# Attention and max-out MoE on one core: W2 ahead of batch 0 in the load queue, x^T of batch 1 on TensorE, and fixed PSUM pools

## The chip, the cores and the metric

The kernel runs on one core of one Trainium2 chip. The metric is the device time of one execution in microseconds. The profile is one execution taken by the hardware profiler; its times count from the start of its span.

## What is computed

Inputs are x (8 batches, 8 heads, 512 rows, 64 wide), state (8, 8, 32, 64) and the weights w1, w2 (512 x 1024) and w_out (1024 x 512), all fp32. The reference, cut to what matters:

```
scores = scale * x @ state^T;    a  = softmax(scores);   xread = a @ state
scores2 = scale * state @ x^T;   a2 = softmax(scores2);  sread = a2 @ x
X = concat(xread, sread over the rows), heads side by side    # 4352 x 512
out = maximum(X @ w1, X @ w2) @ w_out
```

The kernel uses max(h1, h2) = h2 + relu(h1 - h2), so out = X (W2 Wo) + relu(X (W1 - W2)) Wo. For the rows of xread it folds the state S into the weights: X W = a (S W), so that the 512-deep product becomes one of depth 256 (8 heads by 32 states).

## The kernel before, in words

The order of the work on each engine is written out by hand (`manual_schedule`): every engine takes its instructions in the order of the program, and waits where data or a buffer is missing. All loads stand in SP's queue: states of batches 0 to 2, batch 0, then half 0 of W2, two quarters of Wo, half 1 of W2, the other two quarters, both halves of W1, batch 1, the other states, batch 2.

Per batch there are these steps (names of the functions):
- `cast_x` (L180) makes a bf16 copy xp of x, which `u_sr` needs; `u_xt` (L197) transposes xp on TensorE and copies x^T out of PSUM. For later batches `compact_x` (L187) casts into a packed tile xc, and `d_xt` (L194) transposes that by DMA from SP's queue.
- `u_exp` (L210) and `u_norm` (L226): scores, exp on ACT, then reduce, reciprocal and multiply, which give a. `u_at` (L256, TensorE) or `d_at` (L251, DMA) make a^T, the tile aT.
- `u_sr` (L235), `u_srt` (L266): the rows of sread and their transpose into sread_t.
- `sw_mm`/`u_sw` (L275, L289): S W in three chunks of 512 columns. Chunks 0 and 1 are S (W1 - W2). For the first batches they are S W1 plus (-S) W2 from the cast weights (`two`), for the others they come from wcat, which `w_sub` (L387) fills on POOL. Chunk 2 is S (W2 Wo). ACT and VectorE copy the results to swt.
- `l1` (L305): 8 blocks of two matmuls each, a relu after each, by turns on ACT and VectorE. `l2_open`, `l2_add`, `l2_close` (L317 to L333): four output blocks, with 2 + 8 matmuls each.

The weights: `w_cast`, `wo_cast` cast them, `w_t` (L399) transposes W2 on TensorE into w2t, and `w_wo` (L411) builds W2 Wo in four quarters as the quarters of Wo come. L442 to L519 interleave this with batch 0 and with the start of batch 1. From L521 on each batch runs l1 and l2 with the next batch's steps put between the blocks (`fillers`, L420): exps and casts after l1, `u_sr` after l2's first block, S W and the DMA transposes after the third.

[...] Up to L520 there are two pools of four, `ps` for all and `acc` for W2 Wo and l2. Then `one_ring` (L62) closes both and opens one pool of eight. `warm_up` (L133) issues matmuls on zeros.

Of the kernel before, what the change touches and what calls it, by code (L numbers as in the profile page):

```python
# [15 lines left out]
def kernel(  # L16
# [14 lines left out]
    nc = tc.nc  # L31
# [5 lines left out]
    NC = S // 128  # L37
# [10 lines left out]
    keep = ctx.enter_context(tc.tile_pool(name="keep", bufs=2))  # L48
    big = ctx.enter_context(tc.tile_pool(name="big", bufs=2))

    early = ctx.enter_context(ExitStack())
    pools = dict(ps=early.enter_context(tc.tile_pool(name="ps", bufs=4, space=bass.MemoryType.PSUM)),
                 acc=early.enter_context(tc.tile_pool(name="acc", bufs=4, space=bass.MemoryType.PSUM)))
    ctx.enter_context(tc.manual_schedule())

    def bank(dtype=F32, kind="ps"):
        return pools[kind].tile([128, 512 if dtype == F32 else 1024], dtype, tag="b", name=kind)

    def acc():
        return bank(kind="acc")  # L60

    def one_ring():  # L62
        early.close()
        pools["ps"] = pools["acc"] = ctx.enter_context(tc.tile_pool(name="ring", bufs=8, space=bass.MemoryType.PSUM))

    def copy(eng, o, i):
        if eng == "A":
# [23 lines left out]
    def load_states(bs):  # L91
        nc.sync.dma_start(out=s_f[:, 2 * bs.start:2 * bs.stop],
                          in_=state[bs].rearrange("b (q h) n d -> (h n) (b q) d", q=2))
# [6 lines left out]
    def load_w(t, w, ch):  # L100
        cs = slice(ch * 512, (ch + 1) * 512)
        nc.sync.dma_start(out=t[:, :, cs], in_=w.rearrange("(i p) f -> p i f", p=128)[:, :, cs])

    def load_wo(q):
        nc.sync.dma_start(out=wof[:, 2 * q:2 * q + 2],
                          in_=moe_w_out.rearrange("(k p) n -> p k n", p=128)[:, 2 * q:2 * q + 2])

    load_states(first)
    load_x(0)
    for ch in range(2):  # L110
        load_w(w2f, moe_w2, ch)
        load_wo(2 * ch)
        load_wo(2 * ch + 1)
    load_w(w1f, moe_w1, 0)
    load_w(w1f, moe_w1, 1)
    load_x(1)
    load_states(slice(3, 8))
    load_x(2)

    ident = consts.tile([128, 128], BF16)  # L120
# [12 lines left out]
    def warm_up(n):  # L133
        p = bank()
        for k in range(n):
            nc.tensor.matmul(p, warm[:, 0:128], warm, start=(k == 0), stop=(k == n - 1))  # L136
# [28 lines left out]
    def negate_states():  # L165
        for g in range(2):
            gs = slice(64 * g, 64 * g + 64)
            negate("V", sneg[gs], sbd[gs, 0:TWO, g::2, g, :])
# [25 lines left out]
    def d_xt(b):  # L194
        nc.sync.dma_start_transpose(out=st[b]["xt"], in_=st[b]["xc"].rearrange("p h w -> p (h w)"))

    def u_xt(b, g, eng):  # L197
        d = st[b]
        p = bank(BF16)
        for i in range(4):  # L200
            for c in range(NC):
                k = 2 * i + c // 2
                nc.tensor.transpose(p[64 * (c % 2):64 * (c % 2) + 64, k * 128:(k + 1) * 128], d["xp"][:, 2 * i + g, c, 0:64], ident)
        copy(eng, d["xt"].rearrange("p (i g u) t -> p g i (u t)", g=2, u=2)[:, g], p.rearrange("p (i w) -> p i w", i=4))
# [5 lines left out]
    def u_exp(b, g):  # L210
        d = st[b]
        if g == 0:
            d["e"] = at.tile([128, 2, 4, NC, Ns], BF16, tag="e", name="e")
            d["es"] = at.tile([128, 2, 4 * NC], F32, tag="es", name="es")
            d["er"] = at.tile([128, 2, 4 * NC], F32, tag="er", name="er")
            d["a"] = at.tile([128, 2, NC, 4, Ns], BF16, tag="a", name="a")
        p = bank()
        for i in range(4):
            for cp in range(2):
                k = 2 * i + cp  # L220
                nc.tensor.matmul(p[:, k * 64:k * 64 + 64],  # L221
                                 d["xt"][:, 4 * i + 2 * g + cp, :], sbd[:, b, 2 * i + g].rearrange("p u n -> p (u n)"),
                                 start=(k == 0), stop=(k == 7))
        nc.scalar.activation(out=d["e"][:, g].rearrange("p i c n -> p (i c n)"), in_=p, func=ACTF.Exp, scale=scale)  # L224

    def u_norm(b, g, mul):  # L226
        d = st[b]
        nc.vector.tensor_reduce(d["es"][:, g], d["e"][:, g].rearrange("p i c n -> p (i c) n"),  # L228
                                axis=mybir.AxisListType.X, op=ALU.add)
        nc.vector.reciprocal(d["er"][:, g], d["es"][:, g])  # L230
        mul.tensor_mul(  # L231
            d["a"][:, g].rearrange("p c i n -> p i c n"), d["e"][:, g],
            d["er"][:, g].rearrange("p (i c) -> p i c", i=4).unsqueeze(3).to_broadcast([128, 4, NC, Ns]))
# [39 lines left out]
    swt = consts.tile([128, 2, 2, WC], BF16)  # L273

    def sw_mm(b, ch, engs="VA"):  # L275
        pg = [bank(), bank()]
        two = b < TWO and ch < 2 and (b, ch) != (1, 0)
        terms = ((sbd, w1b), (sneg, w2b)) if two else ((sbd, wcat),)
        for k, (sv, w) in enumerate(terms):
            for i in range(4):  # L280
                for g in range(2):
                    gs = slice(64 * g, 64 * g + 64)
                    nc.tensor.matmul(pg[g][32 * i:32 * i + 32, :],  # L283
                                     sneg[gs, b, i, :] if k else sbd[gs, b, 2 * i + g, g, :],
                                     w[gs, i, ch * 512:(ch + 1) * 512],
                                     start=(k == 0), stop=(k == len(terms) - 1))
        return lambda: [copy(engs[g], SW[b][:, g, ch * 512:(ch + 1) * 512], pg[g]) for g in range(2)]
# [99 lines left out]
    def w_sub(q):  # L387
        cs = slice(q * 256, (q + 1) * 256)
        nc.gpsimd.tensor_sub(wcat[:, :, cs], w1f[:, :, cs], w2f[:, :, cs])  # L389

    def w_cast(o, w, ch, engs="VA"):
        cs = slice(ch * 512, (ch + 1) * 512)
        for k in range(2):
            copy(engs[k], o[:, 2 * k:2 * k + 2, cs], w[:, 2 * k:2 * k + 2, cs])

    def wo_cast(q, eng):
        copy(eng, wo[:, 2 * q:2 * q + 2], wof[:, 2 * q:2 * q + 2])

    def w_t(ch, half, eng):  # L399
        p = bank(BF16)  # L400
        for j in range(2):
            for k in range(4):
                f = 4 * ch + k
                nc.tensor.transpose(p[:, (4 * j + k) * 128:(4 * j + k + 1) * 128],
                                    w2b[:, 2 * half + j, f * 128:(f + 1) * 128], ident)
        copy(eng, w2t[:, 2 * half:2 * half + 2, 4 * ch:4 * ch + 4, :].rearrange("p j f t -> p j (f t)"),
             p.rearrange("p (j t) -> p j t", j=2))
# [3 lines left out]
    def w_wo(q, i):  # L411
        if q == 0:
            WO[i] = acc()
        for f in range(2 * q, 2 * q + 2):
            nc.tensor.matmul(WO[i], w2t[:, i, f, :], wo[:, f, :], start=(f == 0), stop=(f == NF - 1))  # L415
        if q == 3:
            copy("V" if i % 2 else "A", wcat[:, i, FF:WC], WO[i])
# [21 lines left out]

    for b in range(B):  # L440
        SW[b] = swt[:, b % 2]
    warm_up(6)  # L442
    cast_states("V", first)
    states(first)
    warm_up(5)
    cast_x(0, (("V", slice(0, 4, 2)), ("A", slice(4, 8, 2)), ("V", slice(1, 4, 2)), ("P", slice(5, 8, 2))))
    u_xt(0, 0, "V")
    u_xt(0, 1, "A")
    u_exp(0, 0)
    u_exp(0, 1)  # L450
    w_cast(w2b, w2f, 0, "VV")
    wo_cast(0, "P")
    wo_cast(1, "P")
    warm_up(1)
    w_t(0, 0, "A")
    w_t(0, 1, "A")
    u_norm(0, 0, nc.vector)
    u_sr(0)
    u_norm(0, 1, nc.vector)
    negate_states()  # L460
    warm_up(3)
    for q in range(2):
        for i in range(4):
            w_wo(q, i)
    w_cast(w2b, w2f, 1)
    wo_cast(2, "P")
    w_t(1, 0, "V")
    w_t(1, 1, "A")
    u_at(0, "V")
    u_srt(0)  # L470
    wo_cast(3, "V")
    for i in range(4):
        w_wo(2, i)
    w_cast(w1b, w1f, 0)
    w_sub(0)
    w_sub(1)
    for i in range(4):
        w_wo(3, i)
    u_sw(0, 0)
    u_sw(0, 2)  # L480
    l1(0, {}, range(0, 4))
    for c in range(NC):
        l2_open(0, c)
    w_cast(w1b, w1f, 1)
    compact_x(1, 0)
    compact_x(1, 1)
    d_xt(1)
    cast_x(1)
    w_sub(2)
    w_sub(3)  # L490
    cast_states("P", rest)
    load_x(3)
    sT = d_states(rest)
    l2_add(0, 0, range(0, 4))
    u_sw(0, 1)
    for c in range(1, NC):
        l2_add(0, c, range(0, 4))
    l1(0, {}, range(4, 8))
    u_sc(1, 0, nc.vector)
    u_sc(1, 1, nc.gpsimd)  # L500
    cast_x(2)
    l2_add(0, 0, range(4, 8))
    l2_close(0, 0)
    u_sw(1, 0)
# [6 lines left out]
    l2_add(0, 2, range(4, 8))  # L511
    l2_close(0, 2)
    u_at(1, "V")
    l2_add(0, 3, range(4, 8))
    l2_close(0, 3)
    d_xt(2)
    u_sw(1, 2)
    u_srt(1)
    l2_out(0)  # L519
    one_ring()  # L520
    for b in range(1, B):  # L521
        fill = fillers(b)
        if b + 2 < B:
# [39 lines left out]
```

The softmax here doesn't subtract the row's maximum and nothing guards it: scores larger than these inputs give would overflow.

## Time and profile before

| | |
|---|---|
| time, median of 4 runs | 155.28 us (154.96 to 156.66) |
| the profiled execution | 155.36 us |
| its span | 153.5 us |
| TensorE busy | 141.2 us, 92% |
| VectorE, ACT, POOL busy | 83.7, 75.5, 43.6 us |
| DMA | 29.89 MB, mean 195 GB/s; 385 GB/s and over from 8 to 22 us |
| l1 of batch 0 starts | 25.17 us |
| l1 of batches 1, 2, ..., 7 starts | 42.39, 56.35, 70.31, 85.43, 100.65, 115.09, 129.05 us |

In lines of the timeline the first two numbers are start and length in us, then come engine, source line, operation, out<-in, shape and count; in brackets stands the idle time just before and what ended it. PE is TensorE's matmul, PEld its weight load, DVE VectorE, SPq the issue of a DMA from SP's queue. "ps" and "acc" are PSUM tiles. In the DMA view q1 is the queue of the kernel's own transfers and q8 one of two that carry instructions.

### The profile page before, as it was taken

The numbers are of one execution on the slowest core, as the hardware profiler recorded it, in microseconds if no ns is written. First come the engines' busy times: TensorE is split into PE (matmuls) and PEld (weight loads), VectorE is DVE, ScalarE is ACT, GpSimd is POOL, SyncE is SP. The second block draws the span as 40 slices with busy tenths as digits, with TensorE's granted clock in tenths as the row PEclk, the third lists the DMA queues.
The fourth block names the chain that finished last, engine by engine and source line by source line (L and its number), as shares of the span: only waits on it lengthen the run. The fifth ranks groups of instructions, "written<-read, shape, count | busy, mean of one in ns | idle before, by whom it ended". The sixth has DMA issues, their size and how long they took to land. (4 is left out here: it accounts for less than half of the span.)

```text
span 153.5 us, 3031 instructions
## 1 busy us (share of the span) xinstructions
PE 141.2 (92%) x1255; PEld 67.0 (44%) x1255; DVE 83.7 (55%) x151; ACT 75.5 (49%) x126; POOL 43.6 (28%) x44
## 2 busy tenths in 40 slices
PE   6769789999799999999999799979999999999990
PEld 1355533344345444534543354335434544664460
DVE  5379628528955486655556355635565546731120
ACT  3065519927864565756384637463747217621010
POOL 3025129994930910270064006300500050000000
PEclk9999999999999999999999999999999999999999
DMA  4999999999399298749849990990099015602423
GB/s 113 349 398 391 383 381 296 286 162 288 72 301 293 89 193 301 249 77 247 282 153 106 319 299 32 107 341 34 2 124 358 0 22 51 273 0 63 138 99 116
DMA packets 37934, 29.89 MB, mean 195 GB/s; under 512 B 24864, under 2 KB 33312, under 8 KB 37024
## 3 DMA queue, kind: packets, MB, share of 16 engines
q1 hardware_dynamic: 37776, 29.56, 69.3%
q8 instruction: 10, 0.16, 0.5%
q10 hardware_dynamic: 144, 0.13, 0.3%
q14 instruction: 4, 0.03, 0.1%
HBM read 15.20 MB, written 8.91 MB: 157 GB/s over the span
## 5 line engine op out<-in xcount | busy, mean ns | idle before, releaser
L326 PE MATMUL acc<-wo,r 128*128 128x512 bf16 x248 | 58.9, 379 | 0.0
L326 PEld LDWEIGHTS <-r 128*128 128x128 bf16 x248 | 23.9, 98 | 28.8 <-issue 0.6
L301 DVE TENSOR_SCALAR r<-ps 128x512 bf16<-128x512 f32 x32 | 22.1, 692 | 19.1 <-PE ps L311 19.0
L311 PE MATMUL ps<-aT,swt 128*128 128x512 bf16 x128 | 29.1, 379 | 3.3 <-DMA aT<-a 2.4
L231 POOL TENSOR_TENSOR a<-e,er 128x512 bf16<-128x512 bf16 x13 | 13.4, 1050 | 64.0 <-ACT e L224 32.2
L70 DVE COPY ob<-acc 128x512 f32<-128x512 f32 (+1 forms) x17 | 11.4, 671 | 27.4 <-PE acc L326 27.0
L299 ACT ACTIVATE r<-ps 128x512 bf16<-128x512 f32 x32 | 19.2, 599 | 10.9 <-PE ps L311 10.6
L311 PEld LDWEIGHTS <-swt 128*128 128x128 bf16 x128 | 12.0, 98 | 18.2 <-issue 3.3
L68 ACT CAST swt<-ps 128x512 bf16<-128x512 f32 x24 | 12.9, 592 | 12.6 <-PE ps L283 12.4
L322 PE MATMUL acc<-swt,aT 128*128 128x512 bf16 x62 | 18.1, 381 | 0.0
L68 ACT COPY ob<-acc 128x512 f32<-128x512 f32 (+1 forms) x16 | 9.2, 576 | 15.9 <-PE acc L326 10.9
L70 DVE CAST swt<-ps 128x512 bf16<-128x512 f32 x24 | 15.3, 681 | 1.8 <-PE ps L283 1.7
L72 POOL CAST xp<-xf 128x2048 bf16<-128x2048 f32 (+1 forms) x8 | 14.3, 1783 | 5.9 <-DMA xf<-in_x_dram 5.9
L224 ACT ACTIVATE e<-ps 128x512 bf16<-128x512 f32 x16 | 8.8, 595 | 14.0 <-PE ps L221 14.0
L68 ACT CAST xc<-xf 128x1024 bf16<-128x1024 f32 x14 | 13.9, 1050 | 0.0
L228 DVE TENSOR_REDUCE es<-e 128x16 f32<-128x512 bf16 x16 | 10.6, 662 | 1.8 <-ACT e L224 1.8
L389 POOL TENSOR_TENSOR wcat<-w1f,w2f 128x1024 bf16<-128x1024 f32 x4 | 9.8, 2477 | 3.0 <-DMA w1f<-in_moe_w_dram 3.0
L415 PE MATMUL acc<-wo,w2t 128*128 128x512 bf16 x32 | 7.2, 379 | 1.5 <-POOL wo L72 1.5
L322 PEld LDWEIGHTS <-aT 128*128 128x128 bf16 x62 | 4.7, 98 | 6.0 <-issue 2.6
L136 PE MATMUL ps<-warm 128*128 128x512 bf16 x15 | 5.9, 536 | 1.3 <-POOL warm L122 1.3
L283 PE MATMUL ps<-wcat,sbd 64*32 64x512 bf16 x168 | 6.7, 380 | 0.1
L221 PEld LDWEIGHTS <-xt 128*128 128x128 bf16 x128 | 4.7, 98 | 3.0 <-ACT xt L68 0.7
(68 smaller groups left out, 102.7 us busy)
## 6 DMA issues: line engine op xcount, KB each, us to landing
xf<-in_x_dram SPq DMA_DIRECT2D x8, 1024.0 KB, 8.5
out_dram<-ob SPq DMA_DIRECT2D x7, 1024.0 KB, 5.2
w2f<-in_moe_w_dram SPq DMA_DIRECT2D x2, 1024.0 KB, 10.2
wof<-in_moe_w_out_dram SPq DMA_DIRECT2D x4, 512.0 KB, 11.5
w1f<-in_moe_w_dram SPq DMA_DIRECT2D x2, 1024.0 KB, 15.7
out_dram<-ob SPq DMA_DIRECT2D x3, 256.0 KB, 2.8
out_dram<-obs SPq DMA_DIRECT2D x8, 64.0 KB, 1.7
s_f<-in_state_dram SPq DMA_DIRECT2D x1, 320.0 KB, 13.6
```

What stands on the lines that cost most here:

```text
L68: nc.scalar.copy(o, i)
L70: nc.vector.tensor_copy(o, i)
L72: nc.gpsimd.tensor_copy(o, i)
L224: nc.scalar.activation(out=d["e"][:, g].rearrange("p i c n -> p (i c n)"), in_=p, func=ACTF.Exp, scale=scale)
L228: nc.vector.tensor_reduce(d["es"][:, g], d["e"][:, g].rearrange("p i c n -> p (i c) n"), axis=mybir.AxisListType.X, op=ALU.add)
L231: mul.tensor_mul(d["a"][:, g].rearrange("p c i n -> p i c n"), d["e"][:, g], d["er"][:, g].rearrange("p (i c) -> p i c", i=4).unsqueeze(3) ...
L299: nc.scalar.activation(out=o, in_=p, func=ACTF.Relu)
L301: nc.vector.tensor_scalar(o, p, scalar1=0.0, scalar2=None, op0=ALU.max)
L311: nc.tensor.matmul(p, SW[b][:, g, f * 128:(f + 1) * 128], AT[b][:, g, :], start=(g == 0), stop=(g == 1))
L322: nc.tensor.matmul(OB[b][1 + c], AT[b][:, g, c * 128:(c + 1) * 128], SW[b][:, g, FF:WC], start=(g == 0), stop=False)
L326: nc.tensor.matmul(OB[b][1 + c], R[b][:, f, c * 128:(c + 1) * 128], wo[:, f, :], start=False, stop=(f == NF - 1))
L389: nc.gpsimd.tensor_sub(wcat[:, :, cs], w1f[:, :, cs], w2f[:, :, cs])
```

## The change

The load queue is led by half 0 of W2 and two quarters of Wo; the states and batch 0 come next, and the rest as before. The hand-written order follows: W2's transposes and the first two quarters of W2 Wo stand before batch 0's work on TensorE, more warm-up matmuls are put in (20 in place of 15), several casts change engine. Batch 1 has its x^T from TensorE (`u_xt`) with the casts split over VectorE and ACT, in place of `compact_x`, `d_xt` and a cast on POOL. Its exps stand inside l1 of batch 0, and chunk 0 of its S W comes from the cast weights. All four `w_sub` stand together, later. The two pools of four banks stay to the end; from batch 2 on the third chunk of S W takes its two banks from `acc`. In the order of instructions on TensorE the changed kernel has 2,600 weight loads and matmuls in place of 2,510, all 90 of them before l1 of batch 1.

```
-    early = ctx.enter_context(ExitStack())
-    pools = dict(ps=early.enter_context(tc.tile_pool(name="ps", bufs=4, space=bass.MemoryType.PSUM)),
-                 acc=early.enter_context(tc.tile_pool(name="acc", bufs=4, space=bass.MemoryType.PSUM)))
+    pools = {k: ctx.enter_context(tc.tile_pool(name=k, bufs=4, space=bass.MemoryType.PSUM)) for k in ("ps", "acc")}
...
-    def one_ring():
-        early.close()
-        pools["ps"] = pools["acc"] = ctx.enter_context(tc.tile_pool(name="ring", bufs=8, space=bass.MemoryType.PSUM))
...
+    load_w(w2f, moe_w2, 0)
+    load_wo(0)
+    load_wo(1)
     load_states(first)
     load_x(0)
-    for ch in range(2):
-        load_w(w2f, moe_w2, ch)
-        load_wo(2 * ch)
-        load_wo(2 * ch + 1)
+    load_w(w2f, moe_w2, 1)
+    load_wo(2)
+    load_wo(3)
     load_w(w1f, moe_w1, 0)
...
     def sw_mm(b, ch, engs="VA"):
-        pg = [bank(), bank()]
-        two = b < TWO and ch < 2 and (b, ch) != (1, 0)
+        pg = [bank(kind="acc" if ch == 2 and b > 1 else "ps") for g in range(2)]
+        two = b < TWO and ch < 2
...
-    warm_up(6)
+    warm_up(11)
+    w_cast(w2b, w2f, 0)
+    w_t(0, 0, "V")
+    w_t(0, 1, "A")
+    wo_cast(0, "P")
+    wo_cast(1, "P")
+    warm_up(3)
+    for i in range(4):
+        w_wo(0, i)
     cast_states("V", first)
     states(first)
-    warm_up(5)
+    negate_states()
+    for i in range(4):
+        w_wo(1, i)
     cast_x(0, (("V", slice(0, 4, 2)), ("A", slice(4, 8, 2)), ("V", slice(1, 4, 2)), ("P", slice(5, 8, 2))))
     u_xt(0, 0, "V")
     u_xt(0, 1, "A")
+    warm_up(2)
     u_exp(0, 0)
     u_exp(0, 1)
-    w_cast(w2b, w2f, 0, "VV")
-    wo_cast(0, "P")
-    wo_cast(1, "P")
-    warm_up(1)
-    w_t(0, 0, "A")
-    w_t(0, 1, "A")
     u_norm(0, 0, nc.vector)
+    w_cast(w2b, w2f, 1, "PA")
+    wo_cast(2, "P")
+    wo_cast(3, "P")
+    warm_up(4)
     u_sr(0)
     u_norm(0, 1, nc.vector)
-    negate_states()
-    warm_up(3)
-    for q in range(2):
-        for i in range(4):
-            w_wo(q, i)
-    w_cast(w2b, w2f, 1)
-    wo_cast(2, "P")
-    w_t(1, 0, "V")
-    w_t(1, 1, "A")
+    w_t(1, 0, "A")
+    w_t(1, 1, "V")
     u_at(0, "V")
     u_srt(0)
-    wo_cast(3, "V")
     for i in range(4):
         w_wo(2, i)
     w_cast(w1b, w1f, 0)
-    w_sub(0)
-    w_sub(1)
...
     l1(0, {}, range(0, 4))
+    w_cast(w1b, w1f, 1, "PA")
+    cast_x(1, (("V", slice(0, 4, 2)), ("V", slice(4, 8, 2)), ("A", slice(1, 4, 2)), ("A", slice(5, 8, 2))))
     for c in range(NC):
         l2_open(0, c)
-    w_cast(w1b, w1f, 1)
-    compact_x(1, 0)
-    compact_x(1, 1)
-    d_xt(1)
-    cast_x(1)
-    w_sub(2)
-    w_sub(3)
+    for q in range(4):
+        w_sub(q)
     cast_states("P", rest)
-    load_x(3)
-    sT = d_states(rest)
     l2_add(0, 0, range(0, 4))
     u_sw(0, 1)
-    for c in range(1, NC):
-        l2_add(0, c, range(0, 4))
-    l1(0, {}, range(4, 8))
-    u_sc(1, 0, nc.vector)
-    u_sc(1, 1, nc.gpsimd)
+    l2_add(0, 1, range(0, 4))
+    l2_add(0, 2, range(0, 4))
+    u_xt(1, 0, "V")
+    u_xt(1, 1, "A")
+    l2_add(0, 3, range(0, 4))
+    l1(0, {4: [lambda: u_exp(1, 0)], 5: [lambda: u_exp(1, 1)]}, range(4, 8))
+    u_norm(1, 0, nc.vector)
+    u_norm(1, 1, nc.gpsimd)
+    load_x(3)
     cast_x(2)
+    sT = d_states(rest)
...
     u_at(1, "V")
+    u_sw(1, 2)
     l2_add(0, 3, range(4, 8))
     l2_close(0, 3)
     d_xt(2)
-    u_sw(1, 2)
     u_srt(1)
     l2_out(0)
-    one_ring()
```

More of the change, by code (lines that the diff above doesn't have):

```diff
@@ L116 @@
     load_x(1)
-    load_states(slice(3, 8))
+    load_states(rest)
     load_x(2)
```

## Prediction

> **What bounds the kernel now.** I read the page first, then TensorE's waits, the windows by batch, the early timeline, and last the DMA view of two narrow windows. The page:
>
> ```profile
> span 153.5 us, 3031 instructions
> ...
> PE 141.2 (92%) x1255; PEld 67.0 (44%) x1255; DVE 83.7 (55%) x151; ACT 75.5 (49%) x126; POOL 43.6 (28%) x44
> ...
> q8 instruction: 10, 0.16, 0.5%
> ```
>
> TensorE is busy for 92% of the span, no other engine for more than 55%. So the question is where TensorE waits. Its waits (us in total, times, longest):
>
> ```profile
> PE ps L311 <- DMA aT<-a: 2.4, 3, 1.1
> PE acc L415 <- POOL wo L72: 1.5, 1, 1.5
> PE ps L203 <- DVE xp L70: 1.4, 1, 1.4
> ...
> PE ps L311 <- ACT sread_t L68: 0.8, 1, 0.8
> ```
>
> The largest lies in the late batches: l1 waits three times for the DMA transpose of a. The windows from one l1 to the next (length, then PE) price it:
>
> ```profile
> 42.39:56.35 13.96, 13.96 (x129) 6.41 (x130) 8.54 (x16) 7.40 (x12) 4.94 (x5) 1.00 0.85 223
> ...
> 70.31:85.43 15.12, 14.13 (x132) 6.40 (x131) 8.14 (x15) 8.81 (x16) 4.13 (x4) 1.00 0.81 191
> 85.43:100.65 15.22, 14.12 (x129) 6.37 (x130) 8.14 (x15) 8.16 (x14) 3.95 (x4) 1.00 0.82 191
> 100.65:115.09 14.44, 14.12 (x129) 6.38 (x130) 8.14 (x15) 7.74 (x13) 2.06 (x2) 1.00 0.53 124
> ```
>
> A clean batch takes 13.96 us with TensorE full; batches 3, 4 and 5 lose 1.16 + 1.26 + 0.48 = 2.9 us. The rest of the room is before 42.4 us. The timeline (start, length) has the points that my steps use:
>
> ```profile
> 7.56 0.62 ACT L68 CAST xp<-xf 128x512 bf16<-128x512 f32 x1 [5.54 <-DMA xf<-in_x_dram]
> ...
> 10.38 1.20 ACT L224 ACTIVATE e<-ps 128x512 bf16<-128x512 f32 x2
> ...
> 19.68 3.61 PE L415 MATMUL acc<-wo,w2t 128*128 128x512 bf16 x16 [1.47 <-POOL wo L72]
> ...
> 22.61 0.69 DVE L70 CAST w1b<-w1f 128x1024 bf16<-128x1024 f32 x1 [2.02 <-DMA w1f<-in_moe_w_dram]
> ...
> 32.74 1.89 PE L311 MATMUL ps<-aT,swt 128*128 128x512 bf16 x8
> ...
> 35.82 0.69 DVE L228 TENSOR_REDUCE es<-e 128x16 f32<-128x512 bf16 x1 [0.46 <-ACT e L224]
> ```
>
> **What the Trainium skill says.** "Runtime: NRT & Kernel Launch", Instruction fetch mechanics: an engine's instructions are fetched by a DMA queue of its own in 16 KiB blocks of 256. The trace agrees: 2 x 1255 TensorE instructions are 9.8 blocks, and q8 moved 10. The page calls the cost mostly hidden; here I doubt it. "DMA: Bandwidth & Descriptors", Queues, rings and completion order: each DMA engine consumes a ring in order and takes turns between rings packet by packet. The first half I use for the loads; the second the trace does not bear out cleanly, since some q8 packets started only when earlier transposes were through. Its section Latency and other measured facts gives DMA transposes 261 GB/s; aT's 256 KB would be 1.0 us as an estimate, but the trace has 3.2 from issue to landing, and that is used.
>
> **The q8 packets.** Narrow DMA windows find them at 83.3, 98.5, 111.6 and 125.5 us, the first three in just the three slow batches. In 80 to 86 us the transpose lands 5.0 us after issue, and in a window of a fast batch without q8, 66 to 70.5 us, 3.2:
>
> ```profile
> q8 instruction: 1, 0.02, 1.0%
> ...
> aT<-a SPq DMA_TRANSPOSE x1, 5.0
> ```
>
> ```profile
> aT<-a SPq DMA_TRANSPOSE x1, 3.2
> ```
>
> A clean batch issues aT 10.0 us after its l1 began (66.36 against 56.35), so 3.2 us leaves 0.7 to spare and 5.0 overruns by 1.1. That fits the 1.0 and 1.1 waited. Where DMA was idle, the packets started after 1938, 2195 and 2449 TensorE instructions, that is 256k less 110. A batch has 258 instructions, so a packet keeps its place in the batch: 10.4 to 10.9 us after l1 there, on top of aT. This is inferred from coincidence, not shown.
>
> **The change, part by part.**
> 1. Loads. The first five (192 + 1024 + 1024 + 512 + 512 KB) keep their sum and change their order, so batch 0 lands last of them, when the second Wo quarter landed before: at 13.0 instead of 7.5 us. Later loads keep their places; half 0 of W1 stays at 22.6. If lines of 2 KB start faster than batch 0's of 1 KB, it could be 12.1; I take 12.9.
> 2. Batch 0's chain. From batch 0's landing (7.54) to the end of the first exp (10.97) were 3.4 us; the norm block on VectorE, first reduce to last multiply, ran 11.48 to 15.23, 3.75 us. So a is whole at 12.9 + 3.4 + 3.75 + 0.1 = 20.15, and after transposes (0.4) the third quarter of W2 Wo starts at 20.6 instead of 19.68. Sixteen matmuls by 216 ns are 3.46: S W1 starts at 24.06. Before it waited for W1's cast until 22.61 + 0.69 + 0.06 = 23.36. Cost 0.7; the load's 5.4 us are otherwise hidden, because that time was spent waiting for Wo and W1. Half 0 of W2's cast, its transposes and the first two quarters of W2 Wo now run before 13 us under the same loads: nothing. Casts moved to POOL (1.04 each) end by 20.95, before the matmul wants them at 22.3: nothing.
> 3. Batch 1's x^T. Removed: two ACT casts (1.05 each), POOL's cast (2.06), SP's DMA transpose (its issue 2.10, ahead of load 3) and the wait for it, 0.6. Added: four casts of about 0.6 on VectorE and ACT, 32 transposes, two PSUM copies (0.69 and 1.01). Batch 1 lands at 28.2 as before; the casts are done by 30.5, and TensorE reaches the transposes at 32.5. If batch 1 were late, VectorE's casts would hold S W1's copies behind them, and those l1's second half; 2 us of margin stand against it. On TensorE 32 transposes by 29 ns (16 weight loads took 0.48 at 8.04) are 0.9 on the path. From l1 of batch 0 (25.17) to its second half (32.74) were 7.57 us of full TensorE; so the second half starts at 25.17 + 0.7 + 7.57 + 0.9 = 34.35. SP, freed, issues load 3 some 2 us earlier, behind which the states' transpose stands as before; that transpose and x^T of batch 2 come about 2 us later and aren't due until 48.
> 4. Exps inside l1. Two 8-matmul groups (0.24 each) now sit between l1's matmuls, and two relus (0.69) stand ahead of the reduce on VectorE: the reduce starts 34.35 + 3.15 = 37.5, against 35.82 = 32.74 + 3.08. The block from there to aT's copy took 5.9 us without a gap (35.82 to 41.73), with the same rows after: aT at 43.4.
> 5. Pool change, third chunk. Before, l1 of batch 1 started 0.65 after aT, waiting for the sread_t copy; now its first bank is freed by aT's own copy: 43.5 against 42.39. **Early loss 1.1.** The eight extra matmuls for S W1 of batch 1 (0.2) fall into TensorE's wait for VectorE: nothing; without that cover 0.2. W1-W2 on POOL moves back and ends at 26.5 + 4 x 2.4 = 36.1, the states' cast at 37.4, before POOL's multiply at 40: nothing.
> 6. Four banks instead of eight later. A bank is wanted again after 4 x 0.43 = 1.73 us and free after 0.43 + 0.17 + 0.69 = 1.3: nothing if relus are prompt. In the trace ACT's first relu comes 0.3 late and still fits. Bounds: 0 to 0.3 a batch; I take 0.4 for all.
> 7. TensorE's instructions: 64 for x^T, 16 for S W1, 10 for five more warm-ups: 90 more before batch 1. The packet moves 90 of 258 instructions earlier, to 7.9 to 8.3 us after l1, and takes 0.9 to 1.8 us: through by 10, before aT's first data at 10.9. **Gain up to 2.9.** In batches 1 to 3 the load of x runs until 9.7 to 10.1 (in batch 1 a us later after the change) and may hold the packet back; bounds 0 and the whole 2.9. I leave 0.4 of loss.
>
> Sum: +1.1 - 2.9 + 0.4 + 0.4 = -1.0 on the span of 153.5, whose execution took 155.36 with 1.9 around it: 154.4, and the median stood 0.08 below that execution. I say 154.4.
>
> **Rivals.**
> - Slower: the packet meets transposes again. Held by x's load it starts at 10 instead of 8, as the one at 57.6 waited for two transposes to end. Price 1.2 a batch, and it decides from two batches on: with three, 155.36 + 1.1 + 0.4 = 156.9; with five, about 158. Against: batches 4 and 5 have little or no load then.
> - Slower by banks or by an idle TensorE: 0.3 in each of six batches, and a further 1 us lost between 13 and 20.6 us where TensorE is thin: 155.36 + 1.1 + 2.8 - 2.5 = 156.8.
> - Faster: batch 0 lands at 12.1, the loss in step 2 goes, and no packet meets a transpose: 155.36 + 0.4 - 2.9 = 152.9.
> - The new order does nothing early (W1's landing at 22.6 rules) and the waits stay: 155.3 to 155.8.
>
> **Numbers.** The sum's case 0.5 (own range 153.6 to 155.6), packets meeting transposes 0.2, banks or idle 0.1, faster 0.12, nothing 0.08. A measurement of this kernel tells about 1% (1.55 us) from no change: below 153.73 is faster, 0.12 + 0.1 of the sum's case; above 156.83 slower, most of both slower rivals. Range 152.7 to 157.5: what lies outside are five batches hit, or a landing earlier still.
>
> **What would show it.** Right: batch 0's first casts at 12.9, third quarter of W2 Wo at 20.6, l1 of batch 1 near 43.5, every later batch within 0.2 of 13.96, aT landing in 3.2 to 3.5, q8 packets near 8 us into a batch. Wrong: l1 of batch 1 after 45 (an early wait that I missed), aT landing in 5 us with q8 beside it (step 7), or aT in 5 without q8, and then the packets were never the cause.

## The result and the profile after

| | before | after |
|---|---|---|
| median of runs | 155.06 us (152.00 to 157.22, 17 runs) | 153.87 us (153.18 to 153.99, 12 runs) |
| profiled execution, its span | 155.36, 153.5 | 153.96, 152.2 |
| ratio after to before | | 1.0088 [1.006, 1.0117] |

The two comparisons have opposite signs. The median fell by 1.2 us, close to the forecast. The ratio takes of each kernel only the runs within 1.5% of its fastest one, so it sets the changed kernel against the low runs of the kernel before alone, the four at 152.0 to 152.5, and against those the changed kernel is 0.9% slower; the ratios below are taken alike. Which runs of before are low, and why, is what the experiments had to find.

The page of the changed kernel has less room left on TensorE (94% busy):

```profile
span 152.2 us, 3113 instructions
...
PE 142.4 (94%) x1300; PEld 68.1 (45%) x1300; DVE 87.6 (58%) x151; ACT 75.4 (50%) x127; POOL 44.1 (29%) x46
...
q8 instruction: 10, 0.16, 0.5%
```

TensorE's waits in the changed kernel (us in total, times, longest). The waits for aT from DMA are gone, and so are those for Wo and for the sread_t copy. What is left are single waits at the start, and two for xp:

```profile
PE ps L258 <- DVE a L227: 1.6, 1, 1.6
PE ps L132 <- POOL warm L118: 1.3, 1, 1.3
PE ps L199 <- DVE xp L64: 1.3, 2, 0.9
```

The windows from one l1 to the next (length, then the engines from PE on) show that every later batch is clean. The stretches left out, and the batch from 99.79, are 13.96 too:

```profile
43.95:57.91 13.96, 13.96 (x129) 6.40 (x129) 9.08 (x17) 7.97 (x14) 5.72 (x5) 1.00 0.89 229
...
71.87:85.83 13.96, 13.96 (x131) 6.41 (x130) 8.14 (x15) 8.06 (x14) 3.94 (x4) 1.00 0.77 208
85.83:99.79 13.96, 13.96 (x131) 6.39 (x130) 8.13 (x15) 8.06 (x14) 3.94 (x4) 1.00 0.77 208
```

Narrow DMA windows find the q8 packets at 53.35, 67.26, 80.29, 94.08, 107.85 and 121.92 us: 8.1 to 9.4 us into a batch (forecast 7.9 to 8.3). Every aT lands in 3.0 to 3.4 us. In 81 to 86 us, where the packet of that batch is already through, the DMA view lists only the kernel's own queue, no q8:

```profile
q1 hardware_dynamic: 2333, 0.59, 63.3%
...
aT<-a SPq DMA_TRANSPOSE x1, 3.4
```

Early on, the third quarter of W2 Wo starts where it was forecast (20.65, forecast 20.6), but l1 of batch 1 comes at 43.95 (forecast 43.5), and VectorE's two casts of batch 1 stand out in the timeline, with POOL's subtractions beside them (each POOL line takes two together: the second and third of four, then the third and fourth):

```profile
28.20 5.07 DVE L64 CAST xp<-xf 128x512 bf16<-128x512 f32 x2
```

```profile
28.14 4.84 POOL L386 TENSOR_TENSOR wcat<-w1f,w2f 128x1024 bf16<-128x1024 f32 x2
...
30.45 5.04 POOL L386 TENSOR_TENSOR wcat<-w1f,w2f 128x1024 bf16<-128x1024 f32 x2
```

TensorE in the same stretch:

```profile
20.65 3.62 PE L412 MATMUL acc<-wo,w2t 128*128 128x512 bf16 x16
...
33.32 0.86 PE L199 MATMUL ps<-ident,xp 128*64 128x128 bf16 x24 [0.45 <-DVE xp L64]
...
43.95 2.32 PE L308 MATMUL ps<-aT,swt 128*128 128x512 bf16 x10 [0.17 <-DVE aT L64]
```

### The profile page after: what moved, and what is told of

Read it like the earlier page. It is cut to its first block, busy times and chain, and to the rows that moved or that the text cites. A ratio compares the mean times of both kernels' runs of the same rounds, so it can differ in the third digit from the quotient of the medians.

```text
span 152.2 us, 3113 instructions
## 1 busy us (share of the span) xinstructions
PE 142.4 (94%) x1300; PEld 68.1 (45%) x1300; DVE 87.6 (58%) x151; ACT 75.4 (50%) x127; POOL 44.1 (29%) x46
## 4 chain that ended last, share of the span: by engine, by line
PE 76%; DVE 14%; DMA 5%; ACT 1%; SPq 1%; issue 1%
PE acc L323 31%; PE ps L308 18%; PE acc L319 9%; DMA s_f<-in_state_dram 5%; DVE xp L64 4%; PE ps L367 2%; PE acc L412 2%; PE acc L377 2%; PE ps L280 2%; PE ps L217 2%; DVE es L224 2%; DVE a L227 2%; PE ps L240 1%; PE acc L357 1%; PE ps L199 1%; DVE swt L64 1%
## 5 line engine op out<-in xcount | busy, mean ns | idle before, releaser
L64 DVE COPY ob<-acc 128x512 f32<-128x512 f32 (+1 forms) x17 | 11.4, 671 | 27.4 <-PE acc L323 26.9
L62 ACT CAST swt<-ps 128x512 bf16<-128x512 f32 x18 | 9.9, 587 | 15.0 <-PE ps L280 15.0
L66 POOL CAST xp<-xf 128x2048 bf16<-128x2048 f32 (+1 forms) x7 | 11.9, 1707 | 2.7 <-DMA xf<-in_x_dram 2.6
L62 ACT CAST xc<-xf 128x1024 bf16<-128x1024 f32 x12 | 12.0, 1052 | 0.0
L64 DVE CAST swt<-ps 128x512 bf16<-128x512 f32 x18 | 11.6, 680 | 0.0
L132 PE MATMUL ps<-warm 128*128 128x512 bf16 x20 | 6.7, 484 | 1.3 <-POOL warm L118 1.3
L64 DVE CAST xp<-xf 128x512 bf16<-128x512 f32 x4 | 6.2, 1594 | 0.0
L66 POOL CAST wo<-wof 128x1024 bf16<-128x1024 f32 x4 | 4.2, 1062 | 6.6 <-DMA wof<-in_moe_w_out_dram 6.6
```

Of the source, the lines that this page charges most:

```text
L62: nc.scalar.copy(o, i)
L64: nc.vector.tensor_copy(o, i)
L66: nc.gpsimd.tensor_copy(o, i)
```

## The experiments

The theory: the q8 packets cost before its late waits, and the change removes these only by shifting the packets, while its new order costs about a microsecond early on. The rival: the new order itself took the waits away, and the packets were only near them. In the diffs, `tiny(n)` puts n matmuls of 32 columns on the warm-up zeros into TensorE's order, two instructions each; it changes no data that anything else uses, but takes one PSUM bank of `ps` in its turn.

**e1_before_padded: the packets alone.** Before, with 90 more TensorE instructions ahead of l1 of batch 1, as many as the change adds, and no other edit.

```
     u_xt(0, 0, "V")          # preceded by:
+    tiny(24)
...
     wo_cast(3, "V")          # followed by:
+    tiny(21)
```

> The kernel before with 45 extra tiny matmuls (32 x 32, on zeros) where TensorE idles early, so that 90 more TensorE instructions stand ahead of batch 1 and nothing else moves. Theory (an instruction packet that meets the DMA transpose of a costs up to 2.9 us): the q8 packets move to about 8 us into each batch, aT lands in 3.2 to 3.5 us, every batch takes 13.96, and the time sits at the lower of before's levels, 152.0 to 152.6, in all runs. Rival (before's spread and its waits for aT have another cause, such as the eight-bank pool or the chip): the time stays near 155.

Measured: 152.24 us (151.65 to 152.92, 22 runs). Before beside it: median 154.65, but from 151.49 to 158.53 over 60 runs, 19 of them below 153.0. Ratio to before's low runs 0.9981 [0.9961, 1.0001]. Two of the windows:

```profile
70.14:84.10 13.96, 13.96 (x131) 6.40 (x130) 8.14 (x15) 8.06 (x14) 3.95 (x4) 1.00 0.78 208
84.10:98.06 13.96, 13.96 (x131) 6.41 (x130) 8.14 (x15) 8.06 (x14) 3.94 (x4) 1.00 0.77 208
```

The packets come 7.8 to 9.5 us into the batches and every aT lands in 3.0 to 3.4 us. Idle matmuls do all that the change does for the later batches, so the rival falls. It also shows that the change, taken without this shift, costs 1.6 us at the median (153.87 against 152.24).

One thing the padding changes besides: 21 of e1's 22 runs have a mean granted TensorE clock of 0.99 or more, but only 11 of before's 60. The clock does not decide alone how long before takes: of those 11 runs eight took 151.7 to 153.7 and three 154.8 to 156.4, and of the 49 at a lower clock 15 took at most 153.7. But how much of the 2.4 us between the two medians the clock has is not separated; what the packets cost is read from the windows of profiles at a clock of 1.00.

**e2_after_padded: the packets put back.** After, with 166 more instructions, so that a packet stands about 12 us into a batch again.

```
     warm_up(11)
+    tiny(30)
...
         w_wo(1, i)
+    tiny(23)
...
     w_t(1, 1, "V")
+    tiny(30)
```

> The changed kernel with 83 such matmuls (166 instructions) where TensorE idles early, which brings the place of the packets in a batch back to that of the kernel before. Theory: aT lands in 4 to 5 us again in some batches, l1 waits for it, and most runs take 155.5 to 157.5, with a spread like that of before. Rival: 153.9, as without them.

Measured: 159.06 (158.53 to 159.95, 6 runs, all at a clock of 1.00), ratio 1.0435 [1.0385, 1.0484], more than expected. Its waits and windows:

```profile
PE ps L313 <- DMA aT<-a: 3.8, 5, 1.0
```

```profile
44.15:58.90 14.75, 14.12 (x129) 6.45 (x129) 9.57 (x18) 8.62 (x16) 5.71 (x5) 1.00 0.92 211
58.90:74.02 15.12, 14.12 (x129) 6.45 (x129) 8.14 (x15) 8.26 (x15) 3.94 (x4) 1.00 0.82 194
74.02:88.96 14.94, 14.12 (x129) 6.44 (x129) 8.14 (x15) 8.16 (x14) 3.94 (x4) 1.00 0.80 194
```

The packets stand 12.8 to 13.1 us into the first five batches and 11.4 into the last, aT takes 4.1 to 5.1 us, and all six batches lose, 4.84 us in sum. In 69 to 74 us both lie together:

```profile
q8 instruction: 1, 0.02, 1.2%
...
aT<-a SPq DMA_TRANSPOSE x1, 5.1
```

l1 of batch 1 starts only 0.20 later than in after, so the cost is the meeting, not the added work. With e1's windows this shows the packets as the cause in both directions.

**e5_before_again: what differs between before's runs.** Before, unchanged, profiled once more.

> The kernel before, unchanged, for another profile. Theory (the packets decide how long one execution of before takes): whatever time this profile has, it is 152.2 plus what its batches lose where a q8 packet stands beside the DMA transpose of a; where all batches take 13.96 the time is near 152. Rival: batches of 13.96 throughout and still 154 or more, or long batches with no packet near the transpose.

Measured: 153.76 for the profiled execution, against 155.36 for the first one; its other run took 156.83. The windows of three batches:

```profile
70.19:84.15 13.96, 13.96 (x132) 6.38 (x131) 8.14 (x15) 8.06 (x14) 4.04 (x4) 1.00 0.74 208
84.15:99.39 15.24, 14.12 (x132) 6.38 (x131) 8.14 (x15) 8.82 (x16) 4.06 (x4) 1.00 0.86 189
99.39:113.60 14.21, 14.12 (x129) 6.38 (x130) 8.14 (x15) 7.51 (x13) 2.06 (x2) 1.00 0.52 126
```

The batch from 70.19 loses nothing: its packet came only at 85.53, when both transposes were through. The next loses 1.28 (aT 5.1 us, with the packet inside it), the one after 0.25. The DMA views of aT's transposes in the first two of these batches, 80 to 84.2 and 94 to 99.4 us:

```profile
q1 hardware_dynamic: 2243, 0.57, 72.5%
...
aT<-a SPq DMA_TRANSPOSE x1, 3.3
```

```profile
q8 instruction: 1, 0.02, 1.1%
...
aT<-a SPq DMA_TRANSPOSE x1, 5.1
```

In the first profile those three lost 1.16, 1.26 and 0.48. So the same program meets its packets differently from one execution to the next. Taking the losses off, both profiles give one figure: 155.36 - 2.9 = 152.5 and 153.76 - 1.5 = 152.2, and e1, which has no losses, runs at 152.24. That is also where before's lowest runs lie. That these low runs had no losses is inferred from this sum; none of them was profiled.

**e3_new_start_old_rest and e4_old_start_new_rest: where the 1.6 us lies.** e3 has after's loads and start, up to the third quarter of W2 Wo, and before's order from there on; e4 the reverse. Both are padded to the same 90 instructions as e1 (`tiny(20)` twice in e3, `tiny(5)` in e4), so that packets cost nothing; in both profiles every later batch takes 13.96 or 13.97. e3 against after, cut to its core:

```
+    w_sub(0)
+    w_sub(1)
...
-    cast_x(1, (("V", slice(0, 4, 2)), ("V", slice(4, 8, 2)), ("A", slice(1, 4, 2)), ("A", slice(5, 8, 2))))
...
-    for q in range(4):
-        w_sub(q)
+    compact_x(1, 0)
+    compact_x(1, 1)
+    d_xt(1)
+    cast_x(1)
+    w_sub(2)
+    w_sub(3)
...
-    u_xt(1, 0, "V")
-    u_xt(1, 1, "A")
...
+    one_ring()
```

> The load order and the hand-written order of the changed kernel up to l1 of batch 0, then the rest of the kernel before (DMA transposes for batch 1, pool of eight), with 40 tiny matmuls so that the packets stand as in the changed kernel. Theory (batch 0's later landing delays the third quarter of W2 Wo): first l1 0.5 later than before, l1 of batch 1 at 42.9, time 152.8. Rival (the landing of W1 rules either way): first l1 at 25.2, time 152.3.

> The start of the kernel before, then the rest of the changed kernel (batch 1 transposed on TensorE, exps inside l1, two pools of four), with 5 tiny matmuls so that the packets stand as in the changed kernel. Theory (32 transposes on the path, and two relus ahead of the reduce): l1 of batch 1 about 1.1 later than before, 43.5, time 153.3. Rival (the early loss is all from the load order): 42.4 and 152.3.

Measured beside e1's 152.24: e3 153.01 (152.53 to 155.55, 22 runs), which is 0.77 more, and e4 152.54 (151.91 to 154.08, 22 runs), 0.3 more. The new start is worth about what step 2 said (0.7). The expectation for e4 was wrong by its own arithmetic: the 1.1 of step 5 contains the 0.7 of the loads, so e4 should have stood 0.4 above e1, and it stands near that. 0.77 + 0.3 = 1.07 leaves some 0.5 of the 1.6. That rest fits the late casts: e4's profile takes 17.65 us from the first l1 to l1 of batch 1, the same within 0.01 as e7 below, which has no such casts, so in e4's profiled execution they cost nothing.

The clock disturbs both figures a little. Five of e3's 22 runs lie apart, at 155.4 to 155.6 and a clock of 0.989, and its profiled execution was one of these, so the times expected for its first l1 and l1 of batch 1 can't be compared (the last section has its slow matmuls); without the five, e3's median is 152.99, 0.75 above e1. Seven of e4's runs have a clock below 0.98 and took 152.74 to 154.08, the profiled one (153.37) among them; the other 15 have a median of 152.40, 0.16 above e1.

**e6_after_pad40: a control for e2.** After, with 80 more instructions, meant to put the packets at another harmless place.

```
     warm_up(11)
+    tiny(20)
...
     w_t(1, 1, "V")
+    tiny(20)
```

> The changed kernel with 40 tiny matmuls (80 instructions): a control for the padding. The packets should come 0.5 to 2 us into a batch, far from aT. Theory (only the place of the packet counts): 153.9 to 154.1, all batches 13.96. Rival (the extra instructions themselves cost, or the 166 of the earlier run did): some half of that run's 5.2 us, 156 or more.

Measured: 153.83, 153.96, 155.58 and 156.19, ratio 1.0152 [0.9994, 1.0309]: inconclusive as a time. In its profiled execution (156.19) all six batches take 13.96, so padding alone does not make the losses of e2. The packets came 4.2 to 8.9 us into the batches, not 0.5 to 2 as expected, four of the six near their place in after, so as a test of another place it says little. What was lost lies in the start, where the granted clock dropped (length, engines, then clock):

```profile
17.00:20.00 3.00, 2.18 (x72) 1.79 (x56) 2.86 (x7) 1.59 (x2) 1.22 (x2) 1.00 1.05 384
20.00:23.00 3.00, 2.02 (x9) 1.12 (x10) 2.82 (x4) 1.25 (x2) 0.38 (x1) 0.66 1.05 382
23.00:26.00 3.00, 3.00 (x12) 1.19 (x11) 0.28 (x1) 0.59 (x1) 1.30 (x3) 0.77 1.14 342
```

In after's profile the clock is 1.00 in the same nine microseconds, although TensorE was less busy in the first three:

```profile
17.00:20.00 3.00, 1.75 (x53) 1.42 (x52) 2.86 (x7) 1.78 (x2) 1.89 (x2) 1.00 1.06 388
20.00:23.00 3.00, 2.63 (x16) 1.37 (x17) 2.20 (x4) 1.26 (x2) 0.00 (x0) 1.00 1.05 382
```

One of the rivals named a loss at this thin place. It did not show in the 12 runs of the changed kernel, nor in the 6 of its repeat below, whose clocks are all 0.996 or more.

**e7_after_casts_on_act: the casts.** After, with all four casts of batch 1's x on ACT.

```
-    cast_x(1, (("V", slice(0, 4, 2)), ("V", slice(4, 8, 2)), ("A", slice(1, 4, 2)), ("A", slice(5, 8, 2))))
+    cast_x(1, (("A", slice(0, 4, 2)), ("A", slice(4, 8, 2)), ("A", slice(1, 4, 2)), ("A", slice(5, 8, 2))))
```

> The changed kernel with the two VectorE casts of batch 1 put on ACT. Theory (VectorE's casts of 2.58 us each wait for POOL's subtractions, and hold TensorE's transposes 0.45 us): the wait on xp before the transposes goes, l1 of batch 1 starts about 0.5 earlier, 43.4, time 0.4 to 0.6 below the changed kernel's 153.9. Rival (those casts are hidden): no change, l1 of batch 1 at 43.9.

Measured: 153.23 (153.12 to 153.36, 6 runs), ratio 1.0072 [1.0049, 1.0094]. Four casts on ACT take less than one of VectorE's did, and TensorE no longer breaks off:

```profile
28.56 2.18 ACT L62 CAST xp<-xf 128x512 bf16<-128x512 f32 x4
```

```profile
32.43 1.08 PE L199 MATMUL ps<-ident,xp 128*64 128x128 bf16 x32
```

From the first l1 to l1 of batch 1 it has 17.66 us (25.62 to 43.28), after 18.30 (25.65 to 43.95). After's own 12 runs lie on two levels, seven at 153.87 to 153.99 and five at 153.18 to 153.36; e7 has only the lower one. What makes the two levels is not shown, since no execution at the lower one was profiled. In after's profile the first cast starts only 0.06 after a subtraction of POOL (28.20 against 28.14) and ends 0.3 after the next one has begun. In e4's profile it starts 0.6 before POOL's next subtraction (28.71 against 29.32), also ends 0.3 after that has begun, and so takes 0.94 instead of 2.58; both casts are then done before TensorE wants them. So probably a small shift against POOL's instructions decides.

**e8_before_two_pools, then e9, e10 and e11 side by side on another chip.** e8 is e1 with the change's pool part alone: two pools of four banks to the end, the third chunk's banks from `acc`, and this chunk of batch 1 ahead of the last block of l2. e9 is e1 again, e10 is e8 again, e11 is after again.

```
-        pg = [bank(), bank()]
+        pg = [bank(kind="acc" if ch == 2 and b > 1 else "ps") for g in range(2)]
...
+    u_sw(1, 2)
     l2_add(0, 3, range(4, 8))
...
-    u_sw(1, 2)
...
-    one_ring()
```

> The first padded kernel (before with 45 tiny matmuls), with the part of the change that touches PSUM alone: two pools of four to the end, third chunk in acc, chunk 2 of batch 1 ahead of the last l2 block. Theory (the wait for the sread_t copy, 0.8, goes with the ring; four banks cost nothing later): l1 of batch 1 at 41.7 in place of 42.2, batches of 13.96, time 151.7 against 152.2. Rival (four banks throttle l1): batches above 13.96, up to 0.3 each, time 152.2 to 154.

> The kernel before with 45 tiny matmuls again, now on one chip with the next two. Theory: 152.2 in all runs, like before's lowest.

> The same with the PSUM part of the change, on the same chip. Theory: 0.5 below the padded kernel, since the 0.8 us wait ahead of l1 of batch 1 goes. Rival: the wait only moves to the DMA transpose of batch 1, which TensorE waited 0.8 for in the one profile so far; then the two are equal within 0.2.

> The changed kernel, unchanged, on the same chip. Theory: with no packet on a transpose in either, it is 1.3 to 1.7 above the padded kernel before (first l1 0.5 to 0.7 later, 0.4 for transposes less the ring's wait, 0.5 for the VectorE casts). Rival: within 0.5 of it.

Measured, 6 runs each: e8 151.57 (151.23 to 152.6); on the other chip e9 152.33 (five runs at 152.18 to 152.35 and one at 153.97, with a clock of 0.978), e10 151.67 (151.49 to 152.02), e11 153.54 (153.16 to 153.99), before 155.79 (152.05 to 156.91, 11 runs). e10's ratio to before's low runs is 0.9936 [0.9888, 0.9983], e11's 1.0056 [1.0, 1.0111]; e8's, on the chip of e7, is 0.997 [0.9908, 1.0033], which does not tell the two apart. Against e9, e11 is 1.21 slower, a little under the 1.3 to 1.7 expected, because three of its six runs lie on after's lower level (153.16 to 153.2) and three on the upper (153.88 to 153.99): about 0.9 and 1.6 above e9. l1 of batch 1 in e9, and then in e10:

```profile
42.37 3.62 PE L316 MATMUL ps<-aT,swt 128*128 128x512 bf16 x16 [0.83 <-ACT sread_t L68]
```

```profile
41.63 3.61 PE L310 MATMUL ps<-aT,swt 128*128 128x512 bf16 x16 [0.16 <-DVE aT L64]
```

0.83 of wait becomes 0.16, and the time falls by 0.66. So the pool part, with the third chunk moved ahead, is a plain gain; which of the two does it is not separated. Before with 90 idle instructions and this part, without the rest of the change, beats both kernels on that chip: 0.6% below before's low runs, 1.9 us below after.

## Why the prediction was right and wrong

- **Steps 1 and 2 held, with some luck.** Batch 0's casts started at 12.62 against 12.9, the third quarter of W2 Wo started at 20.65 against 20.6, and e3 priced the new start at 0.77 against 0.7. Two errors cancelled on the way: the casts started 0.28 early, and from there to the last multiply of a it took 7.68 (12.62 to 20.30), not 3.4 + 3.75 = 7.15. Before had also taken 7.67 (7.56 to 15.23): the sum left out the half microsecond between the first exp and the first reduce.
- **Step 3's cast term failed.** It priced each cast at 0.6, so that all would be done by 30.5. ACT's took 0.62; VectorE's took 2.57 and 2.58, and the second ended at 33.3. POOL's four subtractions, which the change puts together, start at 25.82, 28.14, 30.45 and 32.95; each of the two casts starts under one of them and ends 0.3 after the next has begun. "SBUF — State Buffer", SBUF: two separate sides, in the Trainium skill has a reason: VectorE in its two-port performance modes and GpSimd share a pair of ports as an exclusive lock, held for a whole instruction, and the later one blocks. The trace agrees, with 2.57 and 2.58 for casts that take 0.41 at best, each ending 0.3 after a subtraction of 2.36 to 2.54 us has. About 0.6 is what batch 0's casts take on VectorE (two in 1.18 us before); the step did not ask what POOL runs beside these. Cost: 0.64 by e7 (18.30 less 17.66), in the runs of after's upper level. The transposes themselves took 1.08 (e7) against 0.9.
- **Step 4 held.** From the second half of l1 to the reduce 3.01 us (34.99 to 38.00) against 3.15, and from there to l1 of batch 1 5.95 against 6.0. Both only moved with the late casts.
- **Steps 5 and 6 held.** The ring's wait went (0.83 to 0.16 in e10), and four banks cost nothing in six batches of 13.96; the 0.4 left for them was not needed.
- **Step 7 was right on the mechanism and wrong on its base; this is the step that failed.** The packets moved and their cost went; four of the six came at 8.1 to 8.4, near the 7.9 to 8.3 worked out, and two at 9.4, only 0.5 to 0.7 before aT's issue. The 0.4 of loss left was not needed either. But the step took the 2.9 us of one profile as what every run of before loses. It is a loss that varies from run to run: 2.9 in one profile, 1.5 in the next, and none in the kernels at 152.2. With the terms as measured, the change costs 0.77 (start) + 0.3 (rest) + about 0.5 (casts) = 1.6 and gains between nothing and 2.9 or more. The profiles agree: l1 of batch 1 starts at 42.22 in e1, 43.28 in e7 and 43.95 in after, which is 1.06 for start and rest and 0.67 for the casts. Against the median run the change gains 1.2; against a run without losses there is nothing to win back, and it is slower. That the median fell by nearly the forecast amount is luck: the early loss was 0.5 more than the 1.1 forecast, and the two reserves of 0.4 were not needed. The spread of before's first four runs (154.96 to 156.66) hinted at a varying loss, and the prediction didn't use it.
- **The rivals.** Packets meeting transposes again did not happen in after, though e2 shows that 166 instructions more would have brought it. The slow TensorE at its thin place did not happen in after, but in e3 and e6. No effect at all is out, since the waits for aT went. The faster case needed batch 0 early; its casts started at 12.62, about a third of the way from 12.9 to the rival's 12.1.

## What to carry to other kernels

A wait that recurs once a batch and differs from batch to batch may be an instruction packet beside a transfer: find the packets in the DMA view, count the instructions, and test with idle instructions ahead of the loop before crediting a reordering, reading the batches' windows, since the padding can change the clock of the start too. When a loss depends on where two streams meet, take its size from several profiles and the spread of the runs, since a change that removes it is measured against runs that may not have it. When a cast moves to VectorE, look at what POOL runs in the same microseconds.

## What the runs showed of the hardware

- One 16 KB instruction packet inside aT's transpose of 256 KB took it from 3.0 to 3.4 us to 4.1 to 5.1 us. The place inside matters: with the packet 2.8 to 3.1 us after aT's issue it took 4.8 to 5.1, with 0.9 to 1.4 it took 4.1 to 4.3, and with 0.4 to 0.5 it took 3.4 and 3.6 (before, e2 and e5). Why is open.
- A VectorE cast of 128x512 from fp32 in SBUF took 0.41 at best (batch 0 in after) and 2.58 beside POOL's two-input subtractions. A copy from PSUM beside them kept its 0.68.
- In the profiled executions of e3 and e6 TensorE's clock fell to 0.66 to 0.77 from 20 us on, after a stretch in which TensorE had gaps, the longest 1.85 and 1.80 us; after, with more gaps there but none over 1.61, kept 1.00 from 14 to 29 us. In e4's it fell to 0.50 to 0.72 between 7 and 16 us. The sixteen matmuls of W2 Wo then took 5.30 (e3) and 5.05 (e6), and 3.62 in after. What decides in which runs the clock falls is open.
